# Entries of 256 bytes in the page lists, one buffer for them, and the copy of the expert number moved to the head of the turn

## The chip, the cores and the metric

The kernel runs on one core of a Trainium2 chip. Its engines are TensorE (PE in the profile, its weight loads PEld), VectorE (DVE), ScalarE (ACT), GpSimd (POOL) and SyncE (SP), which here only issues transfers. The metric is the device time of one execution in microseconds. Three runs of the kernel before gave 2530.7, 2534.3 and 2542.32 us; the median, 2534.3, is what the prediction is compared with.

## What is computed

Two stages follow each other: a long convolution over 4 batches of 10048 tokens with 128 channels, done by FFT, and a mixture of 16 experts (4 groups of 4) over the 40192 tokens.

```python
Uf = np.fft.rfft(x * v, n=2 * S, axis=1)
Hf = np.fft.rfft((np.maximum(pos_emb @ w1, 0) @ w2) * window, n=2 * S, axis=0)
y = np.fft.irfft(Uf * Hf[None], n=2 * S, axis=1)[:, :S, :]
x = (x * y).reshape(B * S, D)
...
g_idx = np.argmax(x @ w_group, axis=1)          # the group of each token
e_idx = np.argmax(xg @ w_expert[g], axis=1)     # its expert in the group
h = np.maximum(xg[mask_e] @ w1[g, e], 0.0)      # 128 -> 1024
out[tok_idx] = combined[:, None] * (h @ w2[g, e])   # 1024 -> 128, weighted
```

## The kernel before

**Stages.** The filter's network and its transform come first (`filter`). Then each batch b passes a loop of 22 steps over channels (`j`, L227), which holds the inverse transform of batch b - 1 and the forward transform of batch b, and a middle stage of 40 steps (L252) with the matmuls `psb` and the product with the filter (`middle`, `back`). A last loop (b = 4) holds only the inverse transform of the last batch. Then come the MoE pages (`work`).

**Routing.** While the loops run, `chosen` and `ranked` find the expert and weight of each token of the batch before, and each token's place in the lists of pages. A page is 256 tokens of one expert; there are 204 pages at most, of which 164 are usual. An entry is two words, the token's number and its weight. The entries of a batch are a tile `en` of 128 partitions x 79 x 2 words, from a pool with two buffers (L154, L247). `put` (L835) scatters one column of 128 entries with one indirect DMA of POOL (L836) to the rows `adr` of the list in DRAM, so a batch takes 79 of them, 316 in all. The scatters are drawn by `scatter(n)`: 3 in each step of the loops of b = 2 and 3 (3 and 4 in turn in the latter), 4 in the last, and one in some steps of the middle stage (L259, L261). Those of the last batch run among the first MoE pages. POOL has its own queue and can run ahead of the loop's other work.

**Lists.** The lists in DRAM are first filled with an index that no token has (`ent`, L456 to L459: two memsets, one DMA). `load_list` (L1033) loads one of four parts of them (pages 0 to 15, 16 to 70, 71 to 108, 109 to 203) once it is complete, with one DMA (L1043) of POOL or, for the last part, of SP; then `addresses` casts the token numbers to indices (L1047, L1049), on POOL for the first part and on DVE for others.

**Pages.** A page gathers its tokens by an indirect DMA (`xg`, L1114), transposes them (`px`), splits them into high and low parts (`xh`, `xl`), and multiplies them with the expert's two weight matrices in three matmuls for each product: `ph` (L1169 to L1171), the relu `hh` on ACT (L1177), its residue `hl` on DVE (L1178), `py` (L1188 to L1190), then `ys` on ACT (L1195), `ptm` (L1202), `os` on ACT (L1209) and an indirect DMA to the output (L1214). The expert's weights come by SP (`ws`, L1107); ACT and DVE split them into `wh` and `wl` (L1150, L1158), in some pages POOL makes one `wl`. `turn` (L973) writes the order of all this by hand for five pages in flight. Near its end, `p3.begin()` (L1092) starts a page: DVE copies the page's expert number to a tile `ep` (L1097), and ACT, DVE and SP read it into a register each (L1099, L1100, L1102), for the addresses of the weights. In `turn`, `p1.relu(4)` stands right before `p3.begin()` and `p1.relu(6)` behind it; the engines keep that order.

Of the kernel before, what the change touches and what calls it, by code (L numbers as in the profile page):

```python
# [12 lines left out]
F32 = mybir.dt.float32  # L13
F32R = mybir.dt.float32r
I32 = mybir.dt.int32
AF = mybir.ActivationFunctionType
ALU = mybir.AluOpType
# [8 lines left out]
SEQ, D, NB, N1 = 10048, 128, 79, 157  # L26
# [28 lines left out]
NLOAD, NPROD, NSPEC, NTT, NY = 5, 5, 5, 5, 5  # L55
BIGID = 65535.0
HALVES = slice(0, 64), slice(64, 128)

# [68 lines left out]
def groups(n, step):  # L127
    return [(i, min(step, n - i)) for i in range(0, n, step)]


class Kernel:
# [56 lines left out]
    def conv(self, ctx, right):  # L188
# [24 lines left out]
        for b in range(self.nbat + 1):  # L213
            last = b == self.nbat
# [12 lines left out]
            for j, (d0, n) in enumerate(groups(120, GI) + [(120, 4), (124, 4)]):  # L227
# [13 lines left out]
                for _ in range(3 if last else 1):  # L241
                    next(routing, None)
                self.scatter(4 if last else 3 + j % 2 * (b == self.nbat - 1))
            made, folded = [], []
            if b > 0:
                oh = self.rp.tile([128, NE, NB], F32, tag="oh", name="oh")
                en = self.entries.tile([128, NB, 2], F32, tag="en", name="en")  # L247
                routing = chain(self.chosen(b - 1, xy, oh, en), self.ranked(b - 1, oh, en))
                if last:
                    for _ in range(CHOSEN):  # L250
                        next(routing)
# [190 lines left out]
    def filter(self, ctx, ahead, made, folded):  # L442
# [12 lines left out]

        ent = fp.tile([128, self.pages.nt, 2], F32, name="ent")  # L456
        nc.gpsimd.memset(ent[:, :, 0], BIGID)
        nc.gpsimd.memset(ent[:, :, 1], 0.0)
        nc.gpsimd.dma_start(d["list"].rearrange("(p t) c -> p t c", p=128), ent)  # L459
        tp = ctx.enter_context(tc.tile_pool(name="filt2", bufs=2, reuse_waits="tile"))  # L460
# [262 lines left out]
    def ranked(self, b, oh, en):  # L723
# [5 lines left out]
        tc.keep_in_program_order(  # L729
            v.tensor_scalar(en[:, :, 0], self.idc, float(b * 128 * NB), None, ALU.add)  # L730
        )
# [103 lines left out]
        def put(t):  # L835
            ins = nc.gpsimd.indirect_dma_start(  # L836
                d["list"],
                bass.IndirectOffsetOnAxis(ap=adr[:, t : t + 1], axis=0),
                en[:, t, :],
                None,  # L840
                bounds_check=pg.nt * 128 - 1,
                oob_is_err=False,
            )
            tc.declare_no_dep(ins.ins, group="list", reason="every row has a place of its own")
            tc.add_to_no_dep_group("list", ins.ins)
            return ins
# [108 lines left out]
    def work(self, pages):  # L955
# [4 lines left out]
        for p in pages[:XG]:  # L960
            if p.xg is None:
                p.gather()
        if pages:
            pages[0].begin()
        for i in range(-2, n + 1):
# [7 lines left out]
    def turn(self, p0, p1, p2, p3, old):  # L973


        none = Idle()
        p0, p1, p2, p3, old = (p or none for p in (p0, p1, p2, p3, old))
        old.leave()
        p1.high(1, 0)
# [53 lines left out]
    def load_list(self, part, queue):  # L1033
# [8 lines left out]
        src = d["list"].rearrange("(p t) c -> p t c", p=128)  # L1042
        queue.dma_start(lst, src[:, t0 : t0 + n])  # L1043

# [41 lines left out]
class Page:  # L1086
    def __init__(self, k, q):
        self.k, self.q = k, q
        self.to = self.of = self.weight = self.xg = None
        self.wh, self.wl, self.hh, self.hl, self.ph = ({}, {}), ({}, {}), [], [], {}  # L1090

    def begin(self):  # L1092

        k, nc = self.k, self.k.nc
        ep = k.sp.tile([1, 1], I32, tag="ep", name="ep", bufs=3)
        k.tc.keep_in_program_order(
            nc.vector.tensor_copy(ep, k.pages.expert(self.q))  # L1097
        )
        self.ea = nc.scalar.value_load(ep, min_val=0, max_val=NE - 1)  # L1099
# [127 lines left out]
def build(nbat):  # L1227
# [17 lines left out]
    d["out"] = nc.dram_tensor("out", (nbat * 128 * NB, D), F32, kind="ExternalOutput").ap()  # L1245
    d["list"] = nc.dram_tensor("list", (Pages(nbat).nt * 128, 2), F32, kind="Internal").ap()
    d["xyd"] = nc.dram_tensor("xyd", (nbat * 128 * NB, D), F32, kind="Internal").ap()
# [63 lines left out]
```

## Time and profile before

| | |
|---|---|
| median of 3 runs | 2534.3 us |
| the profiled execution | 2529.75 us |
| its span, first to last instruction | 2528.0 us |
| mean granted TensorE clock | 0.912 |
| PE busy | 2053.1 us (81%) |
| PEld busy | 1846.6 us (73%) |
| DVE busy | 1719.8 us (68%) |
| ACT busy | 1347.5 us (53%) |
| POOL busy | 1500.5 us (59%) |

The profile is one execution, recorded by the hardware. "Busy" leaves out register, branch and semaphore instructions and the issuing of DMAs, except that POOL's indirect transfers show with the time that POOL spends on them. Shares are means over stages that have different limits, so they don't say what bounds any one of them. "Issue" is idle time that no recorded event explains.

### The profile page before, as it was taken

The page shows a single profiled execution, that of the slowest core. Times are in us where ns is not written, and L with a number is a line of the kernel's source. Part 1 is how long each engine was busy: PE and PEld are TensorE (multiplying, and loading weights), DVE is VectorE, ACT ScalarE, POOL GpSimd, SP SyncE. Part 2 cuts the span into 40 slices and gives each one's busy share as a digit, 9 for nine tenths or more (in the row PEclk, how much of TensorE's full clock was granted, in tenths as well). Part 3 has the DMA queues.
Part 4 walks back from the last instruction along what each step waited for, and adds up shares of the span by engine and source line. Part 5 has one row for each costly group of instructions (what it writes and reads, how often), then busy time and mean ns, then how long its engine had stood idle before and what let it go on. Part 6 is the DMA issues. An engine that isn't in the chain of part 4 may idle for free.

```text
span 2528.0 us, 53511 instructions
## 1 busy us (share of the span) xinstructions
PE 2053.1 (81%) x18062; PEld 1846.6 (73%) x18062; DVE 1719.8 (68%) x3431; ACT 1347.5 (53%) x3005; POOL 1500.5 (59%) x1496
## 2 busy tenths in 40 slices
PE   9989899729996299813989655899999999999987
PEld 8778777607884187712788555888888888888887
DVE  5787778707797077911788623677777777777776
ACT  6733544305442054401677433677777777777776
POOL 2286016860596607674177777866666666666663
PEclk9999999859997599955999866999999999999999
DMA  4899568405773049521433211333333333333332
GB/s 130 296 271 273 148 202 278 126 9 135 252 234 108 10 140 300 166 62 40 152 109 111 74 49 40 111 117 110 113 113 114 114 113 114 114 113 109 111 109 69
DMA packets 201325, 338.65 MB, mean 134 GB/s; under 512 B 38558, under 2 KB 77185, under 8 KB 201040
## 3 DMA queue, kind: packets, MB, share of 16 engines
q1 hardware_dynamic: 159824, 275.64, 35.3%
q0 software_dynamic: 31712, 43.94, 5.6%
q10 hardware_dynamic: 9504, 15.54, 2.5%
q8 instruction: 146, 2.39, 0.4%
q14 instruction: 139, 1.14, 0.2%
HBM read 282.60 MB, written 53.30 MB: 133 GB/s over the span
## 4 chain that ended last, share of the span: by engine, by line
PE 33%; DVE 23%; issue 22%; ACT 8%; POOL 6%; DMA 4%; ACTq 3%; another core or an unknown queue 1%; SPq 0%; DVEq 0%; POOLq 0%
DVE wl L1158 7%; PE psa L301 4%; DVE hl L1178 3%; ACT wh L1150 3%; PE psb L371 3%; PE ph L1171 2%; DMA xv<-xv_in 2%; PE ph L1170 2%; PE ph L1169 2%; PE pbp L544 2%; ACTq L1099 2%; PE py L1190 2%; ACT ys L1195 2%; PE po L605 2%; PE py L1188 2%
## 5 line engine op out<-in xcount | busy, mean ns | idle before, releaser
L1178 DVE SCALAR_TENSOR_TENSOR hl<-ph,hh 128x512 fp32r<-128x512 f32 x656 | 451.1, 688 | 307.7 <-ACT hh L1177 262.4
L1177 ACT ACTIVATE hh<-ph 128x512 fp32r<-128x512 f32 x656 | 408.1, 622 | 364.6 <-PE px L1130 214.8
L1114 POOL DMA_INDIRECT xg<-xyd,of x328 | 388.6, 1185 | 229.9 <-PE px L1130 160.4
L1214 POOL DMA_INDIRECT out<-os,to x328 | 366.2, 1117 | 148.6 <-ACT os L1209 78.5
L1190 PE MATMUL py<-hh,wl 128*128 128x256 f32 x1312 | 378.5, 289 | 39.4 <-issue 27.0
L1188 PE MATMUL py<-hh,wh 128*128 128x256 f32 x1312 | 405.0, 309 | 0.3 <-issue 0.3
L836 POOL DMA_INDIRECT list<-en,adr x316 | 320.8, 1015 | 109.9 <-issue 88.3
L1169 PE MATMUL ph<-xh,wh 128*128 128x256 f32 x1312 | 377.9, 288 | 3.6 <-ACT xh L1137 2.6
L1170 PE MATMUL ph<-xl,wh 128*128 128x256 f32 x1312 | 377.6, 288 | 2.4 <-issue 2.4
L1171 PE MATMUL ph<-xh,wl 128*128 128x256 f32 x1312 | 377.6, 288 | 1.8 <-issue 1.4
L1189 PE MATMUL py<-hl,wh 128*128 128x256 f32 x1312 | 377.0, 287 | 1.0 <-issue 1.0
L533 POOL TENSOR_TENSOR y<-t 128x256 f32<-128x256 f32 (+1 forms) x160 | 119.4, 746 | 342.6 <-DVE t L532 340.0
L1190 PEld LDWEIGHTS py<-hh,wl 128*128 128x128 f32 x1312 | 257.2, 196 | 41.3 <-issue 28.4
L1169 PEld LDWEIGHTS ph<-xh,wh 128*128 128x128 f32 x1312 | 258.5, 197 | 4.4 <-ACT xh L1137 2.9
L1171 PEld LDWEIGHTS ph<-xh,wl 128*128 128x128 f32 x1312 | 257.8, 196 | 3.8 <-issue 2.9
L1189 PEld LDWEIGHTS py<-hl,wh 128*128 128x128 f32 x1312 | 258.3, 197 | 2.0 <-issue 2.0
L1170 PEld LDWEIGHTS ph<-xl,wh 128*128 128x128 f32 x1312 | 257.9, 197 | 0.7 <-issue 0.7
L1188 PEld LDWEIGHTS py<-hh,wh 128*128 128x128 f32 x1312 | 257.3, 196 | 1.1 <-issue 1.1
L1158 DVE TENSOR_TENSOR wl<-mw,wh 128x512 fp32r<-128x512 f32 x328 | 228.9, 698 | 0.3
L1150 ACT CAST wh<-ws 128x512 fp32r<-128x512 f32 x328 | 213.8, 652 | 12.6 <-remote 6.0
L1158 DVE TENSOR_TENSOR wl<-ws,wh 128x512 fp32r<-128x512 f32 x288 | 200.1, 695 | 23.0 <-ACT wh L1150 5.5
L1150 ACT CAST wh<-mw 128x512 fp32r x328 | 214.8, 655 | 0.0
(228 smaller groups left out, 4300.6 us busy)
## 6 DMA issues: line engine op xcount, KB each, us to landing
ws<-m_w SPq DMA_DIRECT2D x328, 256.0 KB
ht<-hspec SPq DMA_DIRECT2D x156, 256.0 KB
xv<-xv_in SPq DMA_DIRECT2D x131, 288.0 KB
bt<-c_b SPq DMA_DIRECT2D x95, 256.0 KB
bp<-c_bp SPq DMA_DIRECT2D x76, 256.0 KB
xyd<-xy SPq DMA_DIRECT2D x57, 256.0 KB
xo<-x_out ACTq DMA_DIRECT2D x60, 237.0 KB
hspec<-hs SPq DMA_DIRECT2D x19, 512.0 KB
```

Source lines behind the costliest of these rows:

```text
L1114: ins = nc.gpsimd.indirect_dma_start(self.xg[:, h], None, self.src, bass.IndirectOffsetOnAxis(ap=self.of[:, h : h + 1], axis=0), bounds_ch ...
L1150: k.fix(k.nc.scalar.copy(hi, self.matrix(i, half, self.ea)))
L1158: v.tensor_tensor(lo, self.matrix(i, half, self.ed), self.wh[i][half].bitcast(F32), ALU.subtract)
L1169: k.fix(nc.tensor.matmul(ph[:, j], wh, self.xh, start=True, stop=False))
L1170: k.fix(nc.tensor.matmul(ph[:, j], wh, self.xl, start=False, stop=False))
L1171: k.fix(nc.tensor.matmul(ph[:, j], wl, self.xh, start=False, stop=True))
L1177: k.fix(nc.scalar.activation(hh, ph, AF.Relu))
L1178: k.fix(nc.vector.scalar_tensor_tensor(hl, ph, 0.0, hh.bitcast(F32), ALU.max, ALU.subtract))
L1188: k.fix(nc.tensor.matmul(self.py, wh, self.hh[c], start=(c == 0), stop=False))
L1189: k.fix(nc.tensor.matmul(self.py, wh, self.hl[c], start=False, stop=False))
L1190: k.fix(nc.tensor.matmul(self.py, wl, self.hh[c], start=False, stop=(c == NC - 1)))
L1214: ins = k.nc.gpsimd.indirect_dma_start(k.d["out"], bass.IndirectOffsetOnAxis(ap=self.to[:, h : h + 1], axis=0), o[:, h], None, bounds_chec ...
```

## The change

A row of the list in DRAM takes 64 words (`WIDE`) instead of 2. An entry's scatter writes all 64, from a source that begins at the entry and runs on over the entries behind it; only the first two words of a row are read later. For that the tile `en` is 31 entries longer; its end is set to zero on DVE, and it has one buffer instead of two. The scatters are drawn 4 in each step in every loop. The fill writes a 256-byte row for each entry: 34 DMAs from a tile of 12 rows a partition. The list loads pick two words of each row. And the copy of the expert number becomes a method of its own, `number`, which `turn` calls first of all.

```diff
-                self.scatter(4 if last else 3 + j % 2 * (b == self.nbat - 1))
+                self.scatter(4)
...
-                en = self.entries.tile([128, NB, 2], F32, tag="en", name="en")
+                en = self.entries.tile([128, NB + WIDE // 2 - 1, 2], F32, tag="en", name="en", bufs=1)
+                nc.vector.memset(en[:, NB:], 0.0)
...
-        ent = fp.tile([128, self.pages.nt, 2], F32, name="ent")
+        m = 816 // WIDE
+        ent = fp.tile([128, m, WIDE], F32, name="ent")
+        nc.gpsimd.memset(ent, 0.0)
         nc.gpsimd.memset(ent[:, :, 0], BIGID)
-        nc.gpsimd.memset(ent[:, :, 1], 0.0)
-        nc.gpsimd.dma_start(d["list"].rearrange("(p t) c -> p t c", p=128), ent)
+        lists = d["list"].rearrange("(p t) c -> p t c", p=128)
+        for t0, n in groups(self.pages.nt, m):
+            nc.gpsimd.dma_start(lists[:, t0 : t0 + n], ent[:, :n])
...
-                en[:, t, :],
+                en[:, t : t + WIDE // 2].rearrange("p t c -> p (t c)"),
...
         if pages:
+            pages[0].number()
             pages[0].begin()
...
         p0, p1, p2, p3, old = (p or none for p in (p0, p1, p2, p3, old))
+        p3.number()
         old.leave()
...
-        queue.dma_start(lst, src[:, t0 : t0 + n])
+        queue.dma_start(lst, src[:, t0 : t0 + n, 0:2])
...
+    def number(self):
+        k = self.k
+        self.ep = k.sp.tile([1, 1], I32, tag="ep", name="ep", bufs=3)
+        k.fix(k.nc.vector.tensor_copy(self.ep, k.pages.expert(self.q)))
+
     def begin(self):
-        k, nc = self.k, self.k.nc
-        ep = k.sp.tile([1, 1], I32, tag="ep", name="ep", bufs=3)
-        k.tc.keep_in_program_order(
-            nc.vector.tensor_copy(ep, k.pages.expert(self.q))
-        )
+        k, nc, ep = self.k, self.k.nc, self.ep
...
-    d["list"] = nc.dram_tensor("list", (Pages(nbat).nt * 128, 2), F32, kind="Internal").ap()
+    d["list"] = nc.dram_tensor("list", (Pages(nbat).nt * 128, WIDE), F32, kind="Internal").ap()
```

## Rows read from the trace of the kernel before

**Rows 1.** The page's part on the chain that ended last: shares of the span by engine.

```profile
PE 33%; DVE 23%; issue 22%; ACT 8%; POOL 6%; DMA 4%; ACTq 3%; another core or an unknown queue 1%; SPq 0%; DVEq 0%; POOLq 0%
```

**Rows 2.** The table by stretch for six stretches: the stretch and its length, then for PE, PEld (weight loads), DVE, ACT and POOL busy us and instructions, then the granted TensorE clock, the share of the DMA engines and GB/s. The first four are the inverse loops of b = 1 to 4, the fifth the MoE pages among which the last batch is scattered, the sixth the MoE pages after that.

```profile
235.00:361.00 126.00, 114.33 (x1592) 99.72 (x1592) 98.22 (x197) 64.52 (x114) 8.23 (x12) 0.96 0.58 157
448.00:654.00 206.00, 136.47 (x1599) 108.56 (x1597) 108.59 (x223) 64.12 (x113) 93.75 (x93) 0.77 0.34 95
741.00:951.00 210.00, 132.94 (x1588) 110.81 (x1588) 115.93 (x246) 63.49 (x113) 101.96 (x98) 0.76 0.34 93
1041.00:1225.00 184.00, 87.75 (x1087) 69.07 (x1085) 71.32 (x143) 41.28 (x70) 96.19 (x96) 0.70 0.26 78
1420.00:1600.00 180.00, 98.69 (x582) 92.77 (x581) 60.24 (x108) 61.91 (x134) 141.17 (x137) 0.72 0.19 52
1655.00:2500.00 845.00, 768.45 (x6228) 743.85 (x6227) 654.41 (x1198) 624.86 (x1440) 550.77 (x470) 1.00 0.36 111
```

**Rows 3.** The scatters of entries (L836) grouped, asked for once in each stretch in which they run, in order of time: number, shortest, median and longest duration in ns, start of the first and of the last.

```profile
L836 POOL DMA_INDIRECT list<-en,adr x60: 983/985/1418, 484.1 to 561.8; - x60
...
L836 POOL DMA_INDIRECT list<-en,adr x19: 998/999/1303, 665.9 to 714.4; - x19
...
L836 POOL DMA_INDIRECT list<-en,adr x63: 980/980/2457, 792.4 to 875.0; - x63
...
L836 POOL DMA_INDIRECT list<-en,adr x16: 995/997/1307, 962.7 to 1003.2; - x16
...
L836 POOL DMA_INDIRECT list<-en,adr x79: 983/985/1022, 1074.8 to 1175.5; - x79
```

**Rows 4.** The timeline of PE from 541 to 548: start, duration, instruction, and in brackets the idle time before it and what ended it.

```profile
541.91 0.37 PE L564 MATMUL pt<-ident,z 128*32 128x128 f32 x1 [2.43 <-issue]
```

**Rows 5.** The timeline of POOL in the same stretch.

```profile
541.21 0.98 POOL L836 DMA_INDIRECT list<-en,adr  x1 [0.30 <-issue]
```

**Rows 6.** The table by stretch for ten microseconds inside the first burst (columns as in rows 2).

```profile
534.00:544.00 10.00, 1.12 (x3) 0.53 (x4) 0.00 (x0) 0.00 (x0) 7.56 (x9) 0.50 0.02 1
```

**Rows 7.** Group of the copy of the expert number (L1097) on DVE from 1655 to 2502: columns as in rows 3.

```profile
L1097 DVE COPY ep<-epgi x120: 130/131/133, 1660.9 to 2501.3; 1x1 int32<-1x1 int32 x120
```

**Rows 8.** The timeline of one steady page, all engines (the last matmul of ph that the relu hh needs, the copy ep, the relu, the last matmul ahead of ptm, and ptm).

```profile
2210.01 0.28 PE L1171 MATMUL ph<-xh,wl 128*128 128x256 f32 x1
...
2211.12 0.13 DVE L1097 COPY ep<-epgi 1x1 int32<-1x1 int32 x1
...
2212.02 0.60 ACT L1177 ACTIVATE hh<-ph 128x512 fp32r<-128x512 f32 x1 [1.82 <-PE px L1130]
2212.03 0.28 PE L1190 MATMUL py<-hh,wl 128*128 128x256 f32 x1
...
2212.93 0.44 PE L1202 MATMUL ptm<-ident,ys 128*128 128x128 f32 x2 [0.62 <-ACT ys L1195]
```

**Rows 9.** The chain of that page, followed back from the end of the stretch, in order of time: start, us, what.

```profile
2210.52 0.68 DVE hl L1178
2211.28 0.36 ACTq L1099
...
2217.54 0.69 DVE hl L1178
```

**Rows 10.** The timeline of POOL in the early pages that follow the last scatter.

```profile
1589.04 1.07 POOL L1114 DMA_INDIRECT xg<-xyd,of  x1 [0.16 <-DVE to L1047]
...
1595.66 1.04 POOL L1114 DMA_INDIRECT xg<-xyd,of  x1 [0.16 <-issue]
...
1602.14 1.04 POOL L1114 DMA_INDIRECT xg<-xyd,of  x1 [0.16 <-issue]
```

**Rows 11.** The DMA view of 520 to 560, inside the first burst: the queue that POOL's transfers use (packets, MB, share of 16 engines) and how many it issued.

```profile
q0 software_dynamic: 992, 0.03, 2.0%
...
list<-en,adr POOLq DMA_INDIRECT x32
```

**Rows 12.** The DMA view of 1800 to 1840, in steady pages: the same queue.

```profile
q0 software_dynamic: 720, 1.46, 10.5%
```

**Rows 13.** The first matmul line of the middle stage (L371) grouped, once for each of the middle stages of b = 1 to 3: columns as in rows 3. The first and last starts bound the stage.

```profile
L371 PE MATMUL psb<-z,bt x158: 379/379/483, 361.4 to 448.5; 128*128 128x256 f32 x158
...
L371 PE MATMUL psb<-z,bt x158: 379/379/483, 654.0 to 741.8; 128*128 128x256 f32 x158
...
L371 PE MATMUL psb<-z,bt x158: 379/379/483, 951.7 to 1040.7; 128*128 128x256 f32 x158
```

**Rows 14.** The chain around the last list load, in order of time.

```profile
1585.65 2.13 DMA lst<-list
```

**Rows 15.** The list loads (L1043) grouped on POOL, with what ended its idle time ahead of one of them.

```profile
L1043 POOL DMA_DIRECT2D lst<-list x3: 585/602/620, 1008.4 to 1587.0; - x3
...
  PE px L1130: 74.6, 1
```

**Rows 16.** Two other loads on POOL, of 288 runs each (L340), grouped.

```profile
L340 POOL DMA_DIRECT2D v<-xv_in x2: 692/694/695, 91.2 to 113.2; - x2
```

**Rows 17.** Another load on POOL, of 576 runs (L337), grouped.

```profile
L337 POOL DMA_DIRECT2D x<-xv_in x1: 794/794/794, 90.4 to 90.4; - x1
```

**Rows 18.** POOL's groups from 0 to 60: p of the filter's network, with busy time, mean ns and the idle time before it.

```profile
L385 POOL TENSOR_TENSOR p<-pt,p 128x384 fp32r<-128x384 f32 x14 | 14.3, 1028 | 15.9 <-ACT p L384 14.7 <-PE psh L392 1.2
```

More of the change, by code (lines that the diff above doesn't have):

```diff
@@ L56 @@
 BIGID = 65535.0
+WIDE = 64
 HALVES = slice(0, 64), slice(64, 128)
@@ L729, in ranked @@
         tc.keep_in_program_order(
-            v.tensor_scalar(en[:, :, 0], self.idc, float(b * 128 * NB), None, ALU.add)
+            v.tensor_scalar(en[:, :NB, 0], self.idc, float(b * 128 * NB), None, ALU.add)
         )
```

## The prediction, made before the changed kernel ran

> **What bounds the kernel now.** I read the chain of work that ended last, then the busy table cut at the kernel's stages, then each stage at the level of single instructions. In the chain [rows 1] the reader should see that TensorE holds only a third of it and "issue" a fifth: time in which an engine waits for nothing that the profile can name. The stage table [rows 2] says where. The first inverse loop, which issues no scatters, keeps TensorE busy 114.33 of 126 us. The next two do the same kind of work in 206 and 210 us, with GpSimd busy for half of it. The fourth loop (184 us) and the first ten or so MoE pages (1420 to 1600) are thin too; the long steady stretch of MoE pages has TensorE at 768.45 of 845 us.
>
> *The loops.* The scatters of entries come in bursts of 60, 63 and 79, at (561.8 - 484.1)/59 = 1.32, 1.33 and 1.29 us apart, and smaller remainders of 19 and 16 run in the middle stages [rows 3]. Inside a burst TensorE retires a 0.37 us transpose after 2.43 us of "issue" [rows 4], one each 2.80 us, beside GpSimd's 0.98 us scatters with 0.30 us between them [rows 5]. In ten such microseconds TensorE is busy 1.12, DVE and ACT not at all, and the granted clock is 0.50, the lower of its levels [rows 6]. This stall, not a lack of work, makes a loop some 80 us longer than the first.
>
> *A steady page.* The copies of the expert number come (2501.3 - 1660.9)/119 = 7.06 us apart [rows 7], and two neighbours in the chain, hl at 2210.52 and at 2217.54, 7.02 [rows 9], the period that I use. In one page [rows 8] ACT's relu hh of 2212.02 comes after 1.82 us of idle time, although the last matmul that it needs was issued at 2210.01. The row names px as what ended the wait, but px is no input of hh. The chain [rows 9] names what did: DVE's hl of the relu before (0.68 us), then ACT's sequencer at L1099 (0.36 us). There ACT reads the expert number into a register, ahead of the relu; the read needs the copy L1097, which is queued on DVE behind that hl and runs only at 2211.12. The late relu makes ys late, and for ys TensorE's first ptm waits: 0.62 us in the row, 0.78 counted from the matmul before (2212.93 - 2212.03 - 0.12).
>
> **The change part by part.** *The copy, moved first.* `number()` puts it at the head of the turn, some five microseconds before its readers. It remains 0.13 us of DVE, where DVE idles anyway, and ACT's read then waits for nothing. What is late next? TensorE without its gap has 6.24 to 6.40 us of work in a page. By the steady row [rows 2], over 845/7.02 = 120 pages, DVE is busy 5.4 us a page, ACT 5.2, GpSimd 4.6 and four gaps of 0.30 us: 5.8. So TensorE ends last, at about 6.3, and 120 pages x 0.72 = **-86 us**. Bounds: -94 (the whole 0.78), and -56, if the period stops at the 6.62 and 6.48 us that xg shows in the early pages, where GpSimd is full with wl added to its transfers [rows 10]. Those early pages can gain nothing from DVE; the few that mix both give -3.
>
> *The wider entry.* What does the stall hang on? The DMA engines aren't full: in 40 us of burst 32 scatters of 128 rows take 2.0% of 16 engines [rows 11], 12.8 us of engine time or 3.1 ns a row of 8 bytes; the rows of 512 bytes of the MoE pages, 1.46 MB or 2850 rows, take 10.5% [rows 12], 23.6 ns each. A row of 256 bytes lies between, so the bursts would take 2 to 15%: room enough. What is dense is GpSimd's issuing, one indirect transfer each 1.29 us. In the middle stages the same 8-byte scatters, (1003.2 - 962.7)/15 = 2.7 us apart [rows 3], harm nothing: the middle stages of b = 1 to 3 take 87.1, 87.8 and 89.0 us with 0, 19 and 16 of them [rows 13]. So I take the stall to follow the density of the transfers and not their bytes; the change leaves that as it is: **0**. Its bounds are rival B and, for a row that costs 20 ns more, nothing on the path while the engines stay under 15%.
>
> A rule speaks on this: the Trainium skill, "DMA: Bandwidth & Descriptors", Specifications, has transfers under 512 bytes done as read-modify-write. By it a 256-byte entry would still be in the slow class, and if that is the cause the stall stays, with the same sum; no row here holds a 256-byte entry, so the trace can't settle it.
>
> *Four scatters in each step.* The bursts start 36 and 51 us into their loops [rows 3, 13], and 60 of three a step means 20 steps, 63 of three and four in turn means 18. So 60 becomes 79 and 63 becomes 72: 19 + 9 = 28 scatters leave a stage that doesn't feel them for a burst that stalls, 28 x 1.29 = **+36 us** (0 without a stall); the middle stages get back **-2**. Seven of the second batch stay in the middle. With one buffer the memset of the next entry tile waits for them on DVE, with the router's work of the next batch behind it, and for that nobody waits soon: **+4** (0 to 7 x 2.7 = 19).
>
> *The four list loads.* In the new layout the two words that a load wants lie 256 bytes from the next two, so it takes 128 x 32, 110, 76 and 190 pieces of 8 bytes where it had 128 runs; on 16 engines 256, 880, 608 and 1520 each, 3264 in all. Now the last takes 2.13 us to land on the chain [rows 14], with DVE's cast and then the gathers behind it. A piece costs 3.1 ns if it is like the scatters' rows, 23.6 ns if it is like the 512-byte rows; the former also has 8 bytes, so 3264 x 3.1 = 10 us, with the bound at 77. GpSimd's issue grows as well: 0.60 us for 128 runs [rows 15], 0.69 for 288 and 0.79 for 576 [rows 16, 17], 0.43 ns a run more, so +1.7, +6.0 and +4.1 us for the three loads on its queue; before the second GpSimd sat idle 74.6 us [rows 15], which covers it; the third holds up the gathers. With this **+14 us** (bounds 5, if the second is wholly covered, to 77). SP's queue carries the fourth load, and the weights ws of the next pages are queued behind it.
>
> *The fill of the lists.* 34 issues, at 0.60 us as for the other transfers of 128 runs, take the place of one: 20 us on GpSimd at the start, between its p of L385, which leave it 15.9 us of idle time beside 14.3 busy [rows 18]; 13 MB more go out. **+6 us** (0 to 20).
>
> **Sum.** -86 - 3 + 0 + 36 - 2 + 4 + 14 + 6 = -31 us. On the profiled execution's 2529.75 that is 2499. This execution lies 4.55 us below the median of 2534.3, so the median becomes 2503.
>
> **Rivals.** *B: the 8-byte writes are the cause and 256 bytes cure it.* For it: the only dense runs of such writes are where TensorE stalls. Against it: idle DMA engines. Then a loop ends with GpSimd's own 79 x 1.29 = 102 us, begun 34 to 51 us in, so at 136 to 144 us: -70, -66 and, for the fourth of 184 us, -46; the 36 us aren't paid. The first MoE pages stay as they are, full of GpSimd's transfers. -31 - 36 - 182 = -249: **2285**.
> *C, slower: a piece of a list load costs as much as a 512-byte row.* The loads stand on the path and hold back gathers and weights: +77 for +14, +32 in all: **2566**. It turns the sum positive from about 13 ns a piece ((14 + 31 - 4)/3264). For it: each piece is a transfer of its own. Against it: the scatters' rows of the same 8 bytes.
> *D: the copy's gain ends early*, because GpSimd's transfers set 6.55 us or because px does belong to what ACT waits for: -56 for -86: **2533**, no change.
>
> **How the numbers follow.** Forecast 0.60, B 0.18, C 0.13, D 0.09. The forecast's own range by its bounds, without C and D, is 2475 to 2540. To hold 8 in 10 the range takes B's time in and most of C's: 2275 to 2562. About 0.5% (12.7 us) can be told from no change here, so faster means under 2521.6. Of the forecast 0.43 lies there, 0.14 within and 0.03 above; B is all faster; of C 0.10 is slower and 0.03 within; of D 0.03 is faster, 0.03 within and 0.03 slower. Faster 0.64, same 0.20, slower 0.16.
>
> **What the profile after would show.** The copy is judged by the steady page: no relu behind the register read, copies 6.3 us apart; 6.55 says D. TensorE's lone transposes each 2.8 us in bursts of 79, 72 and 79 say that the stall is one of density; loops of some 140 us say B. The list loads are read at their landings and at the waits of DVE's L1047: over 30 us there is C. Idle time ahead of DVE's memset shows the one buffer, and TensorE waiting for p the fill. The prediction is wrong above all if the stall depends on the bytes of a row, since no row here shows any but 8 bytes that dense.

## The result, and the profile after

The changed kernel takes 2548.72 us (median of 7 runs, 2544.58 to 2556.14), the kernel before 2532.77 on the same chip: a ratio of 1.0063, with a 95% interval from 1.0043 to 1.0083. So it loses 0.6%, 16 us, little but clear of noise, where 2503 us and a gain were forecast. The profiled executions have spans of 2528.0 and 2546.9 us.

The reader should see first that the loops with scatters are as thin as before, and longer. The table by stretch of the changed kernel (columns as in rows 2; the loops of b = 2, 3 and 4, and steady pages), and the fourth loop of the kernel before once more:

```profile
456.00:687.00 231.00, 135.25 (x1595) 108.06 (x1593) 108.76 (x222) 63.99 (x113) 109.56 (x111) 0.74 0.34 95
774.00:994.00 220.00, 135.66 (x1602) 110.72 (x1600) 117.12 (x244) 63.76 (x113) 110.32 (x106) 0.75 0.35 99
1088.00:1300.00 212.00, 110.86 (x1349) 83.98 (x1347) 86.87 (x206) 59.32 (x122) 97.41 (x98) 0.73 0.32 104
1760.00:2500.00 740.00, 708.63 (x5848) 697.86 (x5846) 619.28 (x1125) 600.26 (x1350) 505.05 (x448) 1.00 0.39 120
```

```profile
1041.00:1252.00 211.00, 110.89 (x1346) 83.96 (x1344) 86.19 (x203) 59.29 (x122) 96.79 (x97) 0.73 0.29 93
```

The fourth stretch of [rows 2] ends at 1225, before the stage does: it holds 1087 matmuls, where the stage up to the first copy of the expert number has some 1346. So its 184 us, which the prediction and some expectations use, is too short; the like of the changed kernel's 212 us is 211, and this stage didn't grow.

The middle stages, whose first and last starts bound the loops (answering to [rows 13]; in the first line both passes over L373 are counted):

```profile
L373 PE MATMUL psb<-z,bt x316: 379/379/631, 83.0 to 243.6; 128*128 128x256 f32 x158
...
L373 PE MATMUL psb<-z,bt x158: 379/379/483, 368.5 to 455.6; 128*128 128x256 f32 x158
...
L373 PE MATMUL psb<-z,bt x158: 379/379/483, 687.1 to 774.2; 128*128 128x256 f32 x158
...
L373 PE MATMUL psb<-z,bt x158: 379/379/634, 993.9 to 1088.4; 128*128 128x256 f32 x158
```

The scatters of the loops of b = 2 and 3 and the rest in the third middle stage (to [rows 3]):

```profile
L841 POOL DMA_INDIRECT list<-en,adr x79: 982/982/1432, 491.8 to 593.6; - x79
...
L841 POOL DMA_INDIRECT list<-en,adr x72: 980/982/2461, 824.6 to 919.4; - x72
...
L841 POOL DMA_INDIRECT list<-en,adr x7: 997/998/1299, 1005.1 to 1021.4; - x7
```

And PE's timeline inside the first burst (to [rows 4]):

```profile
546.64 0.42 PE L303 MATMUL psa<-fa,eo 96*64 96x158 f32 x1 [2.38 <-issue]
549.44 0.42 PE L303 MATMUL psa<-fa,eo 96*64 96x158 f32 x1 [2.38 <-issue]
```

The bursts are 79 and 72 long, 1.31 and 1.34 us apart, seven scatters are left for the middle stage, and TensorE again retires one matmul each 2.80 us. The group of the last 116 copies of the expert number (to [rows 7]):

```profile
L1103 DVE COPY ep<-epgi x116: 130/131/134, 1758.3 to 2514.2; 1x1 int32<-1x1 int32 x116
```

They lie (2514.2 - 1758.3)/115 = 6.57 us apart, where they lay 7.06. Then the fill (34 issues of GpSimd in the place of one), the first list load on GpSimd with its first use, and the chain at the last two loads (to [rows 14, 15]):

```profile
L464 POOL DMA_DIRECT2D list<-ent x34: 540/540/601, 11.5 to 56.4; - x34
```

```profile
1029.09 1.77 POOL L1050 DMA_DIRECT2D lst<-list  x1 [5.92 <-issue]
...
1037.86 0.21 POOL L1054 CAST to<-lst 128x32 int32<-128x32 f32 x1 [4.88 <-DMA lst<-list]
```

```profile
1691.17 22.48 DMA lst<-list
```

What DVE waits for, in the changed kernel (us in total, times, longest), and its wait for lists in the kernel before:

```profile
DVE to L1054 <- DMA lst<-list: 31.5, 3, 12.4
DVE en L249 <- DMA list<-en,adr: 5.1, 1, 5.1
```

```profile
DVE to L1047 <- DMA lst<-list: 10.1, 1, 10.1
```

Cut at the middle stages and at the copies of the expert number, this is where the time went. The two columns at the right are a pair of runs that the experiments bring (e5_before, e6_after), on a chip where the kernel before is faster; they come into play below.

| stretch (us) | before | after | difference | difference on the other chip |
|---|---|---|---|---|
| start to the end of the middle stage of b = 0 | 235.8 | 243.6 | +7.8 | +6.8 |
| loop of b = 1 | 125.6 | 124.9 | -0.7 | +1.7 |
| loop of b = 2 | 205.5 | 231.5 | +26.0 | +51.6 |
| loop of b = 3 | 209.9 | 219.7 | +9.8 | +1.2 |
| middle stages of b = 1, 2 and 3 | 263.9 | 268.7 | +4.8 | +15.9 |
| then to the first copy of the expert number | 210.7 | 211.1 | +0.4 | +61.0 |
| first to 49th copy | 437.6 | 458.8 | +21.2 | -23.9 |
| 49th to last copy (115 pages) | 812.3 | 755.9 | -56.4 | -94.3 |
| last copy to the end (the copy stands earlier in its turn) | 26.7 | 32.7 | +6.0 | +6.3 |

### The profile page after: what moved, and what is told of

It is laid out like the page before. It is cut to its first block, busy times and chain, and to the rows that moved or that the text cites. A ratio compares the mean times of both kernels' runs of the same rounds, so it can differ in the third digit from the quotient of the medians.

```text
span 2546.9 us, 53567 instructions
## 1 busy us (share of the span) xinstructions
PE 2057.2 (81%) x18062; PEld 1857.3 (73%) x18062; DVE 1734.3 (68%) x3435; ACT 1368.6 (54%) x3005; POOL 1503.8 (59%) x1529
## 5 line engine op out<-in xcount | busy, mean ns | idle before, releaser
L1186 ACT ACTIVATE hh<-ph 128x512 fp32r<-128x512 f32 x656 | 398.3, 608 | 265.1 <-PE ph L1180 105.2
L1123 POOL DMA_INDIRECT xg<-xyd,of x328 | 381.7, 1164 | 220.0 <-PE px L1139 145.1
L1223 POOL DMA_INDIRECT out<-os,to x328 | 357.5, 1090 | 137.1 <-issue 55.8
L1178 PE MATMUL ph<-xh,wh 128*128 128x256 f32 x1312 | 380.2, 290 | 26.5 <-DVE hl L1187 23.9
L1167 DVE TENSOR_TENSOR wl<-ws,wh 128x512 fp32r<-128x512 f32 x288 | 219.4, 762 | 48.5 <-ACT wh L1159 22.7
L303 PE MATMUL psa<-fa,eo 96*64 96x158 f32 x2048 | 192.2, 321 | 41.7 <-issue 32.9
```

Source lines behind the costliest of these rows:

```text
L1123: ins = nc.gpsimd.indirect_dma_start(self.xg[:, h], None, self.src, bass.IndirectOffsetOnAxis(ap=self.of[:, h : h + 1], axis=0), bounds_ch ...
L1167: v.tensor_tensor(lo, self.matrix(i, half, self.ed), self.wh[i][half].bitcast(F32), ALU.subtract)
L1178: k.fix(nc.tensor.matmul(ph[:, j], wh, self.xh, start=True, stop=False))
L1186: k.fix(nc.scalar.activation(hh, ph, AF.Relu))
L1223: ins = k.nc.gpsimd.indirect_dma_start(k.d["out"], bass.IndirectOffsetOnAxis(ap=self.to[:, h : h + 1], axis=0), o[:, h], None, bounds_chec ...
```

## The experiments

The chips are of two kinds: the kernel before takes 2312 to 2319 us on some (e1 to e11) and 2530 to 2550 on others (the prediction's, e12 to e14). Each run stands beside the kernel before on the same chip, and ratios are to that; e5, e13 and e14 are one execution each. Comparisons between runs of different chips go by these ratios.

| run | what it is | before | this | ratio (95%) |
|---|---|---|---|---|
| e1_number | before + copy early | 2312.0 | 2204.9 | 0.954 (0.952 to 0.956) |
| e2_wide | changed, copy late | 2312.0 | 2441.5 | 1.056 (1.054 to 1.058) |
| e3_narrow | changed, 8-byte entries | 2312.0 | 2241.1 | 0.969 (0.967 to 0.970) |
| e4_pause | before, 8 memsets behind every scatter | 2312.0 | 2683.6 | 1.159 (1.157 to 1.161) |
| e5_before | before | 2318.7 | 2317.4 | |
| e6_after | changed | 2318.7 | 2340.0 | 1.009 (1.007 to 1.011) |
| e7_two | e3 with two buffers | 2318.7 | 2221.7 | 0.959 (0.957 to 0.961) |
| e8_gpmemset | changed, memset on GpSimd | 2315.5 | 2281.5 | 0.985 (0.984 to 0.987) |
| e9_splists | changed, lists by SP | 2315.5 | 2329.6 | 1.007 (1.005 to 1.009) |
| e10_rows64 | changed, 64-byte rows, two buffers | 2315.5 | 2308.6 | 0.997 (0.996 to 0.999) |
| e11_gap | before, 3 memsets behind scatters of the loops | 2318.6 | 2418.8 | 1.044 (1.041 to 1.047) |
| e12_best | e1, second list's casts on GpSimd | 2541.6 | 2484.9 | 0.979 (0.976 to 0.982) |
| e13_gapnum | e1 + e11 | 2550.2 | 2407.8 | |
| e14_nowrite | before, entries dropped | 2550.2 | 2519.9 | |

**e1_number: the copy alone.**

```diff
+            pages[0].number()
             pages[0].begin()
...
+        p3.number()
         old.leave()
...
+        k.fix(k.nc.vector.tensor_copy(self.ep, k.pages.expert(self.q)))
...
-        k.tc.keep_in_program_order(
-            nc.vector.tensor_copy(ep, k.pages.expert(self.q))
-        )
```

> The kernel before with the copy of the expert number at the head of the turn and nothing else. Theory one (the copy gains what the trace after shows in the steady pages, about 0.5 us for each of 120, and the rest of the 86 us is lost to relus that still come late): 2533 - 60 = about 2473. Rival (the copy is worth the full 86 us, and the wide entries are what makes the relus late in some pages): about 2447, with no page over 6.4 us. Second rival (px, which the rows name, is what relu waits for, and the copy alone does nothing): 2533.

It gains some 105 us on a chip of the faster kind, more than any theory gave it, and its pages tell why. The last 116 copies, of e1_number and of the kernel before on another chip of that kind (e5_before):

```profile
L1098 DVE COPY ep<-epgi x116: 130/130/132, 1458.0 to 2171.0; 1x1 int32<-1x1 int32 x116
```

```profile
L1097 DVE COPY ep<-epgi x116: 130/131/132, 1481.6 to 2288.9; 1x1 int32<-1x1 int32 x116
```

713.0/115 = 6.20 us a page stands against 807.3/115 = 7.02. So the chain that [rows 9] showed was the cause, the whole wait was there to gain, and px, which the rows name, wasn't it. On this kind of chip this version beats the kernel before and the changed one (e6_after).

**e2_wide: all but the copy.**

```diff
-            pages[0].number()
...
-        p3.number()
```

> The changed kernel with the copy back in its old place, so all of the change but the copy. Theory one: 2549 + 60 = about 2609, of which the stages before the MoE pages hold 48 us as in the changed kernel, and the list loads some 30. Rival (the copy is worth 86 us): about 2635.

It is 129 us slower than the kernel before. Between e2_wide and e6_after the copy is worth 4.7%, 108 us. What DVE waits for, in e2_wide (us in total, times, longest):

```profile
DVE en L249 <- DMA list<-en,adr: 120.9, 3, 60.1
```

The memset of the entry tile's tail (L249) holds DVE for 121 us until the scatters of the batch before have landed: the planner put it early in DVE's queue, ahead of the transforms' work.

**e3_narrow: 8-byte entries, the rest of the change kept.**

```diff
-WIDE = 64
+WIDE = 2
...
-                nc.vector.memset(en[:, NB:], 0.0)
```

> The changed kernel with entries of 8 bytes: one constant, so the fill is one transfer again, the list loads are 128 runs, and the memset of the tile's tail falls away; the copy, the four scatters a step and the one buffer stay. Theory one (the bytes matter for the fill, 8 us, and the list loads, 32 us, and not for the bursts): about 2509, loops of b = 2 and 3 still 231 and 220 us. Rival (the 256-byte rows are what makes the loops 26 and 10 us longer): loops back at 206 and 210 us and about 2473.

4.1% less than e6_after: the entry's size, with the memset that it brings, costs some 95 us there, more than the fill and the lists that theory one held responsible. The loop of b = 2, "the second loop" from here on, is 136 us instead of 187, since with the tail the memset is gone. The single buffer still costs: DVE's en at L660 waits 49.7 us for scatters.

**e7_two: e3 with two buffers.**

```diff
-                en = self.entries.tile([128, NB + WIDE // 2 - 1, 2], F32, tag="en", name="en", bufs=1)
+                en = self.entries.tile([128, NB + WIDE // 2 - 1, 2], F32, tag="en", name="en")
```

> e3_narrow (the changed kernel with entries of 8 bytes) with two buffers for the entries again, so that it differs from e1_number by the four scatters a step alone. Theory one (the one buffer is what e3_narrow lost to e1_number, 38 us: DVE waits for the scatters of the batch before, 12 us in each of two middle stages and 12 at the end of the fourth loop): about 2205 where the kernel before takes 2312. Rival (the placement of the scatters is what costs): 2235 to 2241 again.

Between the two theories: 1.0% (23 us) less than e3_narrow, which is the buffer, and 0.4% (some 10 us) more than e1_number, which is the four scatters in each step. No wait for scatters is left on DVE.

**e5_before and e6_after: both kernels on a chip of the faster kind.**

> The kernel before once more, for its profile on the chip of this job. The first four experiments ran on a chip where the kernel before takes 2312 us instead of 2533. Theory one (on such a chip TensorE isn't slowed in the bursts; nothing else differs): about 2312, loops of b = 2, 3 and 4 of about 134, 139 and 106 us, TensorE issuing at full rate while scatters follow each other at 1.3 us, pages 7.02 us apart. Rival (the chip differs in the pages too): pages at another period. Should the job run on a chip like that of the prediction: 2533, with loops of 205, 210 and 184 us.

> The changed kernel, on the same chip as the run of the kernel before. Where TensorE isn't slowed in bursts, theory one gives it e2_wide less the copy's gain there (0.82 us for 119 pages, and some 7 before them): 2441 - 104 = about 2337, pages at 6.20 us, and a wait of DVE's memset for the scatters of the batch before of some 50 us in the second loop. Rival (the change is good on such a chip): below 2300. On a chip like that of the prediction: 2549, pages at 6.59 us.

Theory one held in both. The loops of e5_before (b = 2, 3 and 4), and PE's timeline in its first burst, where GpSimd issues a scatter at 541.25 and the next at 542.54:

```profile
451.00:586.00 135.00, 117.89 (x1597) 102.35 (x1596) 108.55 (x221) 62.83 (x114) 99.37 (x92) 0.92 0.53 144
674.00:811.00 137.00, 119.46 (x1599) 103.28 (x1598) 117.07 (x243) 62.71 (x114) 103.92 (x94) 0.91 0.52 141
902.00:1008.00 106.00, 96.03 (x1346) 76.61 (x1345) 86.92 (x203) 59.88 (x122) 74.96 (x70) 1.00 0.57 185
```

```profile
540.83 1.38 PE L301 MATMUL psa<-fa,eo 96*64 96x158 f32 x18
```

The program and the pitch of 1.29 us are the same, and TensorE isn't slowed at all. The three loops, the fourth with what follows up to the first copy, are 248 us shorter than on the prediction's chip (70.5, 72.7 and 104.6); the first 49 pages take 36 us longer, and 212 us of span are left between the two kinds of chip. The change comes out slower there too, by other terms (right column of the table above): the pages gain 94 us, and the memset's waits give it back in the second loop and ahead of the first page. DVE's waits for scatters in e6_after:

```profile
DVE en L249 <- DMA list<-en,adr: 119.3, 3, 59.3
```

**e8_gpmemset: the memset on GpSimd.**

```diff
-                nc.vector.memset(en[:, NB:], 0.0)
+                nc.gpsimd.memset(en[:, NB:], 0.0)
```

> The changed kernel with the memset of the entry tile's tail on GpSimd instead of DVE; GpSimd's queue holds the scatters that it has to wait for anyway. Theory one (the memset, placed early in DVE's queue, is what makes DVE wait 119 us for the scatters of the batch before, and 50 us of the second loop, 16 of the third middle stage and some 10 before the first page follow from that): second loop back at about 135 us, and some 60 us less than the changed kernel, 2280 where that takes 2340. Rival (any first write to the single buffer waits as long, the router's en among them): the loop stays at 187 us and the time within 15 us of 2340.

2.4% (55 us) less than e6_after, as theory one said; the second loop is 136 us. The waits that remain (the router's own first write to the one buffer, and the lists):

```profile
DVE en L661 <- DMA list<-en,adr: 49.2, 2, 43.6
DVE to L1054 <- DMA lst<-list: 44.3, 3, 25.5
```

**e9_splists: all list loads by SP.**

```diff
-                        ready = self.load_list(0, nc.gpsimd)
+                        ready = self.load_list(0, nc.sync)
...
-                self.ready = self.load_list(part, self.nc.sync if part == 3 else self.nc.gpsimd)
+                self.ready = self.load_list(part, self.nc.sync)
```

> The changed kernel with all four list loads on SP's queue instead of one. On GpSimd three of them take 1.77, 4.38 and 3.22 us to issue. Theory one (the loads cost what their 8-byte pieces take on the DMA engines, about 10.6 ns a piece on each engine, as 22.46 us for the 608 + 1520 pieces of the last two shows): the landings stay, and the time within 10 us of the changed kernel's 2340. Rival (GpSimd's issuing is what holds up the gathers): 15 to 25 us less. Second rival (weights queued behind the loads on SP): 10 to 30 us more.

0.25% (some 6 us) less than e6_after, with intervals that overlap; the last two loads still take 22.70 us on the chain. The time agrees with theory one. A gain from GpSimd's shorter queue and a loss from weights queued behind the loads could also cancel, and this run doesn't part them. What it shows by itself is how the pieces travel. The DMA view of the last two loads (1516 to 1540; queue, packets, MB, share of 16 engines):

```profile
q1 hardware_dynamic: 34224, 0.53, 121.3%
```

34,048 of these packets are the pieces of the two loads, one piece each.

**e10_rows64: 64-byte rows and two buffers.**

```diff
-WIDE = 64
+WIDE = 16
...
-    tag="en", name="en", bufs=1)
+    tag="en", name="en")
```

> The changed kernel with rows of 64 bytes (a quarter of the bytes, as many pieces in the list loads) and with two buffers for the entries, which fit at this size; so it differs from e7_two by the entry's size, the fill and the list loads alone, and no memset waits. Theory one (the number of pieces sets the price of the list loads, 3264 x 10.6 ns = 35 us on the path, beside some 4 us for a fill of 3.3 MB): about 0.958 + 39/2318, a ratio of 0.975, 2260 where e7_two takes 2222. Rival (the 256-byte stride is what is dear): within 10 us of e7_two. Second rival (any entry over 8 bytes slows the scatters): scatters over 1.45 us apart, loops longer than 140 us.

No theory held: 0.997 instead of 0.975. Two buffers didn't end the memset's wait (61.3 us on DVE, the second loop 187 us instead of 133), because the planner sets the third tile's memset ahead of work of the second. For the lists it tells what it was meant to. Beside e7_two the first 49 pages take 34.3 us more (483.6 for 449.3), and DVE's wait for lists grows as much (first e7_two, then e10_rows64):

```profile
DVE to L1053 <- DMA lst<-list: 45.1, 2, 31.5
```

```profile
DVE to L1054 <- DMA lst<-list: 79.6, 3, 47.9
```

That agrees with theory one's 35 us on the path. The chain at the last two loads in e7_two (8-byte rows), e10_rows64 (64) and e8_gpmemset (256):

```profile
1426.65 2.39 DMA lst<-list
```

```profile
1501.37 22.54 DMA lst<-list
```

```profile
1468.22 22.42 DMA lst<-list
```

The number of pieces sets the price, not the stride: (608 + 1520) pieces on each engine in some 22.5 us are 10.6 ns a piece, in the mean, with the pages' own transfers between them. The Trainium skill, "DMA: Bandwidth & Descriptors", Measured, gives about 10.5 ns a packet for a load of 64 packets issued from GpSimd. That is 0.67 us by the count of the whole transfer, while the 10.6 ns here are time of one engine of 16, so the likeness of the two figures confirms nothing.

**e4_pause and e11_gap: scatters further apart.** Eight memsets behind every scatter, then three behind those of the loops (the second is shown):

```diff
+                for _ in range(pause):
+                    self.mark = ins
+                    ins = self.nc.gpsimd.memset(self.idle, 0.0)
+                    self.behind(ins)
+                    self.mark = ins
```

> The kernel before with eight memsets of 128 x 16 on GpSimd behind each scatter, some 0.1 us each, so that scatters in a burst come about 2.1 us apart. Theory one (TensorE stalls while indirect transfers follow each other at 1.3 us; density): TensorE works on during the bursts, the loops of b = 2 and 3 fall from 206 and 210 us to about 165 (60 to 63 x 2.1 us plus the 36 to 51 us before), the fourth stays near 184 to 200, the MoE pages with scatters lose 79 x 0.8 = 63 us: about 2510. Rival (each scatter of 8-byte rows holds TensorE up by a fixed amount, however far apart): loops stay at 206 us or grow by 0.8 x 60 = 48 us each: 2630 to 2690.

> The kernel before with three memsets of 128 x 16 on GpSimd behind each scatter of the loops only, 0.25 us each as e4_pause measured, so that the scatters there come about 2.05 us apart. On a chip like that of the prediction (the kernel before at 2533 us): if the stall follows the density of the transfers, loops of b = 2 and 3 of at most 170 us instead of 206 and 210; if not, as long as before or longer. On a chip like those of the experiments so far (2312 to 2319 us), where nothing stalls: loops still 134 to 139 us, the middle stages 10 to 25 us longer, because GpSimd's products there queue behind the scatters that are left, and the fourth loop's end 50 us later with its 79 scatters: about 2400.

Both ran on chips that don't stall, so they tell nothing of the stall. They tell the price of a burst that is stretched: loops of 135 to 140 us in both, but middle stages grow, the second from 88 to 186 us in e4_pause, the second and third to 115 and 137 us in e11_gap, because GpSimd's products y stand behind the scatters in its queue (DVE waited 218.9 us for y in e4_pause).

**e12_best: e1 and the casts of the second list on GpSimd.**

```diff
-                self.ready(self.nc.vector)
+                self.ready(self.nc.gpsimd if part == 1 else self.nc.vector)
```

> e1_number (the kernel before with the copy moved and nothing else) with one thing more: the casts of the second list part on GpSimd, behind the load that they wait for, instead of on DVE, where e1_number shows 34 us of waiting for that list with the first pages' work queued behind. Theory (the first pages hold tokens gathered before, so TensorE can work through that wait): 20 to 30 us less than e1_number, a ratio of about 0.942 where e1_number has 0.954. Rival (GpSimd's queue of scatters holds back the gathers, which are late next): within 5 us of e1_number. On a chip like that of the prediction (2533 us): pages at 6.59 us as in the changed kernel there, or at 6.20 if the wide entries made its relus late.

This ran on a chip of the prediction's kind, and takes 2.1% less than the kernel before there. The last 116 copies:

```profile
L1098 DVE COPY ep<-epgi x116: 130/131/133, 1686.2 to 2446.1; 1x1 int32<-1x1 int32 x116
```

759.9/115 = 6.61 us a page with 8-byte entries, and 6.57 in the changed kernel there: what the copy doesn't gain on such a chip isn't due to the wide entries. What the casts do, e12_best leaves open, as e1_number ran on the other kind.

**e13_gapnum and e14_nowrite: density or bytes, on a chip that stalls.** The first is e1_number with three memsets behind each scatter of the loops. The second bounds the rows:

```diff
-                bounds_check=pg.nt * 128 - 1,
+                bounds_check=0,
```

> e1_number with the three memsets behind each scatter of the loops, as in e11_gap, so that scatters there come some 2.4 us apart. On a chip where the kernel before takes 2530 to 2545 us: if TensorE's stall follows the density of the indirect transfers, loops of b = 2 and 3 of at most 175 us instead of 206 and 210; if each scatter costs TensorE a fixed time, or any stream of them does, they stay at 205 to 215 us or grow. Where the kernel before takes 2312 to 2319 us: loops of 134 and 139 us, as without the memsets, and nothing more is learnt.

> The kernel before with a bound of 0 on the rows of the scatters, so that GpSimd issues each of them as before and nearly all of their entries are dropped: it leaves out the writing of the lists, and the pages work on empty lists. On a chip where the kernel before takes 2530 to 2545 us: if GpSimd's issuing is what slows TensorE, loops of b = 2, 3 and 4 stay at 206, 210 and 184 us; if the writes of 8 bytes are, they fall to some 134, 139 and 106 us. Where the kernel before takes 2312 to 2319 us: 134, 139 and 106 us either way.

Both ran on a chip of the prediction's kind (the kernel before at 2550). GpSimd's timeline in the first burst of e13_gapnum, its loops of b = 2, 3 and 4, and the scatters of the fourth (columns as in rows 3):

```profile
526.16 1.10 POOL L842 DMA_INDIRECT list<-en,adr  x1 [0.61 <-issue]
527.25 0.47 POOL L295 MEMSET idle<- 128x16 f32 x3
528.34 0.98 POOL L842 DMA_INDIRECT list<-en,adr  x1 [0.61 <-issue]
```

```profile
448.00:582.00 134.00, 117.47 (x1587) 102.13 (x1587) 108.71 (x223) 63.79 (x113) 99.00 (x209) 0.92 0.53 144
699.00:839.00 140.00, 119.85 (x1592) 103.30 (x1592) 117.19 (x243) 62.76 (x113) 93.86 (x191) 0.90 0.50 137
972.00:1183.00 211.00, 114.56 (x1349) 85.15 (x1347) 86.52 (x204) 58.63 (x122) 125.65 (x335) 0.74 0.29 93
```

```profile
L842 POOL DMA_INDIRECT list<-en,adr x79: 977/979/1337, 1006.5 to 1118.2; - x79
```

With 2.1 us from scatter to scatter, two loops run in 134 and 140 us, as on a chip that never stalls. In the fourth the scatters stay (1118.2 - 1006.5)/78 = 1.43 us apart, and the loop takes 211 us as in the kernel before: a control in the same run. The spacing isn't free: beside the kernel before the two loops gain 140 us, and the middle stages lose 72 of them again (336.2 for 263.9). The loops of b = 2 and 3 of e14_nowrite:

```profile
450.00:654.00 204.00, 131.76 (x1596) 106.74 (x1595) 107.62 (x221) 63.57 (x114) 91.99 (x92) 0.77 0.34 95
744.00:946.00 202.00, 133.56 (x1600) 107.00 (x1599) 117.72 (x242) 64.72 (x114) 100.99 (x96) 0.78 0.35 96
```

They stay slow with entries left out. How much writing this takes away is limited: the DMA view of 520 to 560 still counts as many packets, of fewer bytes (the changed kernel's burst, 540 to 580, in the second fence):

```profile
q0 software_dynamic: 1004, 0.02, 1.9%
```

```profile
q0 software_dynamic: 998, 1.02, 8.2%
```

From 0.02 over 0.03 [rows 11] to 1.02 MB in 40 us the stall is the same; a run with no write at all wasn't made.

## Why the prediction came out wrong

Two terms were mis-sized, the price of the list loads and the gain of the copy, and both errors go the same way. The measured 2549 us lies in the stated 2275 to 2562 only because that range takes in rival C; the forecast's own bounds end at 2540.

**The wider entry, 0: right, and its reason with it.** The stall follows the density of GpSimd's transfers and not their bytes: the changed kernel's bursts of 32 times the bytes stall TensorE alike, and in e13_gapnum the same scatters further apart don't. Rival B is out. What the reason leaves out is that density isn't enough: on the faster chips the same pitch of 1.29 us does nothing. The rule of read-modify-write under 512 bytes, which the prediction set beside it (the Trainium skill, "DMA: Bandwidth & Descriptors", Specifications), isn't what decides the stall: a chip of either kind gets the same small writes, and on one kind nothing stalls.

**Four scatters a step, +36: right on this chip.** 79 and 72 of them in the loops and 7 after, as counted, and the loops of b = 2 and 3 grew by 26.0 + 9.8 = 35.8 us. Where nothing stalls it costs some 10 us (e7_two over e1_number).

**The fill, +6: right in size**, 7.8 us. What in it costs the time is open: the quarter of the bytes, in 8 transfers, lengthens this stretch of e10_rows64 no less (248.4 us for 238.9 in e5_before).

**The copy, -86: the mechanism right, the size too large.** The 115 pages of the table gain 56.4 us, and 120 some 59. The wait behind the register read is gone; e1_number and e6_after, at 6.20 us a page, show that the step was if anything too careful. On the prediction's kind of chip some relus come late again: in the last 116 pages ACT idles over 1 us before 28 of 460 relus (before the change 116), in e1_number and e6_after before none. ACT, PE and GpSimd in one such page of the changed kernel (the last matmul of ph that the relu needs, by the order of `turn`, ACT's cast before it, and GpSimd's four transfers):

```profile
1838.33 0.28 PE L1180 MATMUL ph<-xh,wl 128*128 128x256 f32 x1
```

```profile
1838.77 0.68 ACT L1159 CAST wh<-ws 128x512 fp32r<-128x512 f32 x1
1841.39 1.26 ACT L1186 ACTIVATE hh<-ph 128x512 fp32r<-128x512 f32 x2 [1.94 <-PE py L1199]
```

```profile
1835.65 1.04 POOL L1123 DMA_INDIRECT xg<-xyd,of  x1 [1.37 <-PE px L1139]
1837.00 1.01 POOL L1123 DMA_INDIRECT xg<-xyd,of  x1 [0.31 <-issue]
1838.33 1.02 POOL L1223 DMA_INDIRECT out<-os,to  x1 [0.31 <-issue]
1839.65 1.00 POOL L1223 DMA_INDIRECT out<-os,to  x1 [0.31 <-issue]
```

The relu starts 1.94 us after the cast, while its matmuls were issued at 1838.33 and the py that the row names is no input of it; GpSimd's four transfers follow each other at 1.33 us, the pitch of the bursts. It looks like the same stall on a small scale: pages of 6.2 us pack the transfers closer than pages of 7.0. That is argued from the rows and from its absence on the faster chips; pages with their transfers pulled apart weren't run on a chip that stalls. So the cause of the 27 us that the copy fell short stays open. Rival D named a floor of GpSimd near 6.55 us, and its number is close to what came, but GpSimd isn't full in these pages: 505.05 of 740 us and some 113 x 4 gaps of 0.30 us.

**The list loads, +14: wrong, and this is the step that failed by its reasoning.** The prediction took 3.1 ns for a piece of 8 bytes, by dividing the engines' time by the 4096 rows of 32 scatters. The same row of the DMA view counted 992 packets, 31 for a scatter: its 128 rows don't travel one by one, so time per row there is no price of a transfer of one piece. By packets it gives 12.8 us / 992 = 13 ns, a mean of two kinds (16 packets of 8 rows and some 15 of 4 bytes for each scatter). The DMA view of the changed kernel from 1691 to 1714:

```profile
q1 hardware_dynamic: 24611, 0.69, 105.5%
q0 software_dynamic: 408, 0.55, 31.0%
```

24,320 of the first are the pieces of the fourth load, by SP, one piece each. The third load has 9,728 pieces and GpSimd's queue only 408 packets, with those of its other transfers, so its pieces travel many to a packet; yet the two loads take 22.48 us together, and 22.70 in e9_splists, where both travel by single pieces. So the piece is what has a price, 10.6 ns in the mean of such a stretch, and 3264 pieces are 35 us: 22.48 instead of 2.13 us at the last two loads, and at the first, with a longer issue, 8.8 us (1029.09 to 1037.86) instead of 3.5 in the kernel before (1008.44 to 1011.98). GpSimd's issues of 1.77, 4.38 and 3.22 us were forecast at 2.3, 6.6 and 4.7. DVE's wait for lists grew from 10.1 to 31.5 us, over the 30 us that the prediction named as the sign of rival C. It is half of rival C's price, and its direction. In the table it lies in +5.5 us of the third middle stage and +21.2 us of the first 49 pages.

**The one buffer, +4 (0 to 19): held here, for a reason that the prediction hadn't.** DVE waits 5.1 us for it on the prediction's chip, since there the loops crawl through the bursts anyway. On the faster chips it waits 119 us, far over the bound: the memset stands where the planner puts it in DVE's queue, with work of the transforms behind it. "For that nobody waits soon" was wrong.

In sum: about +35 instead of +14 for the lists makes -10 of the forecast's -31, so the lists alone wouldn't have turned its sign; -59 instead of -86 for the copy makes +17 of that, and the fill's 2 us more +19, by which the profiled executions differ (2546.9 and 2528.0). That it comes out to the microsecond is luck: what the stages hide of the lists isn't measured on this chip.

## What to carry to other kernels

Where a register read stands in an engine's queue ahead of work, put the copy that it needs early on the engine that makes it; one 0.13 us copy behind a 0.7 us operation cost 0.8 us of each page. Price a strided load by its contiguous pieces (10.6 ns on each engine here), and take the price from a load of such pieces, not from the rows of another kind of transfer; a list of 8-byte entries should lie close together. Give a tile that transfers still read a second buffer, keep its first write off the queue that others live on, and if the engines beside a burst of indirect transfers slow down, try spacing it, and count what GpSimd's own later work loses by that.

## What the runs showed of the hardware

The kernel before takes 2312 to 2319 us on some chips and 2530 to 2550 on others, with a granted clock of 0.95 against 0.91 in the mean. On the slower kind TensorE, while GpSimd issues indirect transfers 1.3 us apart, starts one matmul each 0.7 to 1.4 us at first (the kernel before, 506 to 514) and one each 2.80 us later. It recovers within some 10 us: the burst ends at 562.8, and from 569.2 eight matmuls take 2.18 us. At 2.1 us from transfer to transfer it isn't slowed. What the chips have different, and what in a transfer slows TensorE, no run here settles.

One rival stands untested, that the recording of the profile takes part in the stall: every time here is that of a recorded execution. On the slower kind the traces also lack records from the first scatters on. Up to the loop of b = 2 the trace of the kernel before holds 8016 records of semaphore updates, as that of e5_before does; in the loop of b = 2 it holds 1642 against 2426, and in the last 115 pages 8215 against 14,793. The loop of b = 2 of e13_gapnum, which doesn't stall, lacks them too (1789). So the names of what ended a wait are less certain in traces of the slower kind.

A scatter of 128 rows goes out as 31 packets, whether a row has 8 or 256 bytes (992 and 998 packets for the scatters of 40 us), and three memsets of 128 x 16 with their issue cost GpSimd 0.8 us between two scatters.
